# A mixture-of-experts kernel on Trainium2: first expert's index ahead of its low halves, second weights held back, rows of 4160 bytes, six slots transposed by TensorE

## The chip, the cores and the metric

The kernel runs on one core of one Trainium2 chip. The metric is the device time of one execution in microseconds (us). Five engines work side by side, each in the order of its own queue: PE (TensorE, matrix products; PEld is its loading of weights), DVE (VectorE), ACT (ScalarE), POOL (GpSimd, here the issuer of indirect DMAs) and SP (SyncE, the issuer of all other DMAs). An instruction that has to wait stops everything behind it on its engine.

## The reference

Block-local attention (4 batches, 8 heads, 768 positions, 64 channels) gives `x`, 3072 rows of 512. A first expert layer follows: each row goes to one of 8 experts, each takes 384 rows, by a greedy walk over all logits (`flat`, 3072 x 8) in falling order; w1 is 512 x 1024 and w2 1024 x 512 per expert. A second expert layer with a skip gate and a residual ends it.

```python
order = np.argsort(-flat)
for idx in order:
    tok, e = (int(idx) // E, int(idx) % E)
    if assigned[tok] >= 0 or counts[e] >= cap:
        continue
    ...
h = np.maximum(x[mask] @ w1[e], 0.0)
out[mask] = h @ w2[e]
```

## The kernel before, in words

**Precision.** Products are in half precision with a high and a low half: `w1h`, `w1l` are the halves of w1, `hh`, `hl` those of the hidden rows. A product needs three passes: high x high, low x high, high x low. ACT makes the high halves of the weights (L672), DVE the low halves (L675).

**The greedy walk** (`Route.phase`). The experts are closed one after the other. For each, a search of six levels finds the threshold: DVE compares all rows with a level's thresholds (`cmp`, L465), PE counts (L489, L499, L503), DVE takes the next digit (`dg`, `df`, `thr`). At its end `s` (L529) names the expert that closes. From it come `ei` (L547, which lets SP load that expert's weights), masks `bo` (L600), 24 small products on PE (L603), a copy (L606) and an addition (L607) that gives `idx`, the expert's 384 row numbers.

**One expert of the first layer** (`Moe1`). `weights` (L654) loads w1 and w2 in eight pieces of 512 KB into the buffers `wst`, w1 first. `gather` (L678) fetches the rows by three indirect DMAs on POOL (L684, 128 rows each, into `xg`) and transposes them: by DMA (L685), but for expert 0 by PE (L689), with half of each block copied by ACT (L691) and half by DVE (L692). `ffn` (L695) makes eight blocks: `ph` (L708, 3 x 4 products, in two PSUM buffers in turn), `hh` by ACT (L711), `hl` by DVE (L712); then the products `py` (L722) with w2, copied to `yt` (L726). A row of `yt` is 512 values in halves, 512 values and two numbers: 1026 floats, 4104 bytes. It is written to `ysc` in DRAM (L771), and the rows go to `out` by a scatter (L645).

**The second layer** (`Moe2`). List A has six slots of 128 rows, which can start before the last two experts are done, list B the rest. `slot` (L932) gathers rows of `ysc` into `xg` (L934), transposes them by DMA on SP (L940), makes `ph` (L951), `hh`, `hl` (L955), `py` (L962), adds the residual into `xg` (L966) and scatters to `out`. `xg` has four buffers, so a slot's gather waits for the scatter of the slot four before it.

**What sets the order.** All of this is recorded as operations and put in order by a list scheduler (`Sched`): each has an estimated duration, a priority and a correction from a table (`BIAS2` for the expert part) by engine, stage and name. The resulting order of each engine is what runs. Semaphores are set by what an operation reads and writes, not by the table. The key `after` in `weights` is such an estimate only: w2 loads of expert 0 wait for nothing on the chip but their buffers.

Of the kernel before, what the change touches and what calls it, by code (L numbers as in the profile page):

```python
# [427 lines left out]
class Route:  # L428
# [220 lines left out]
class Moe1(Ops):  # L649
# [27 lines left out]

    def gather(self, k, idx, P):  # L678
# [3 lines left out]
        for i in range(3):  # L682
            xg=t([128,1026],F32,"xg",bufs=4); xb=xg.bitcast(F16)[:,:1024]
            self.s.op('POOL',1.1,[idx.name]+[('xscr',c) for c in range(24)],[xg.name],lambda xb=xb,i=i: nc.gpsimd.indirect_dma_start(out=xb,out_offset=None,in_=self.xscr,in_offset=bass.IndirectOffsetOnAxis(ap=idx[:,i:i+1],axis=0)),P-1,dma=.73)  # L684
            if k: self.s.op('SP',.65,[xg.name],[(x.name,i)],lambda xb=xb,i=i: nc.sync.dma_start(x[:,:,128*i:128*i+128],xb,transpose=True),P,dma=1.3)  # L685
            else:
# [338 lines left out]
def build(ctx, tc, i, out, stop=None):  # L1025
# [61 lines left out]
```

## Time and profile before

| | us |
|---|---|
| three runs | 809.8, 813.09 (median), 820.53 |
| profiled execution, own time | 810.57 |
| its span in the profile | 808.7 |
| mean granted PE clock | 0.932 of full speed |

All times of the profile count from the start of the span. A row of a timeline gives the start, the duration, engine, line, operation, what is written and read, and how many instructions it joins; in brackets the idle time of the engine ahead of it and what ended that. The attention ends at about 220 us, the expert part takes the rest.

### The profile page before, as it was taken

How to read it: one execution, taken by the hardware profiler on the slowest of the kernel's cores; microseconds unless marked ns; L12 is line 12 of the kernel's file. 1: busy time of each engine (PE TensorE's matmuls, PEld its weight loads, DVE VectorE, ACT ScalarE, POOL GpSimd, SP SyncE). 2: the span in 40 equal slices, each digit the busy share in tenths (PEclk: the TensorE clock that was granted, in tenths of full speed). 3: DMA queues.
4: the chain of work that ended last, by engine and by line, in shares of the span. 5: the costliest groups of instructions: out<-in, count | busy, mean ns of one | idle time of the engine just before them, and what ended most of it. 6: DMA issues, size and time to landing. Idle time of an engine off the chain costs nothing. (4 is left out here: it accounts for less than half of the span.)

```text
span 808.7 us, 21735 instructions
## 1 busy us (share of the span) xinstructions
PE 698.8 (86%) x8411; PEld 476.8 (59%) x8411; DVE 620.3 (77%) x1875; ACT 402.6 (50%) x777; POOL 229.7 (28%) x233
## 2 busy tenths in 40 slices
PE   3899998978636979998999889799899989999792
PEld 2688877866534545554546454445576657776671
DVE  7888988897685888998999889666569576855740
ACT  3889997864412351525252526452533445646320
POOL 2775866631302011111111113202021132222210
PEclk9999999998755988999999999899999999999997
DMA  8767779691424094868696869999995898898910
GB/s 234 195 162 232 209 215 262 127 175 38 119 90 158 14 300 109 275 169 271 156 266 188 258 183 315 248 298 327 261 220 113 332 344 220 270 324 273 289 31 6
DMA packets 172672, 167.36 MB, mean 207 GB/s; under 512 B 85237, under 2 KB 133365, under 8 KB 172560
## 3 DMA queue, kind: packets, MB, share of 16 engines
q1 hardware_dynamic: 164688, 143.83, 64.6%
q0 software_dynamic: 7872, 22.05, 8.2%
q8 instruction: 68, 1.11, 0.6%
q14 instruction: 44, 0.36, 0.1%
HBM read 114.35 MB, written 29.91 MB: 178 GB/s over the span
## 5 line engine op out<-in xcount | busy, mean ns | idle before, releaser
L708 PE MATMUL ph<-xT,w1h 128*128 128x384 f16 x512 | 102.2, 339 | 7.5 <-DMA xT<-xg 5.1
L951 PE MATMUL ph<-xT,w1h 128*128 128x128 f16 x1152 | 90.1, 222 | 11.6 <-DVE hl L955 7.7
L951 PEld LDWEIGHTS <-w1h 128*128 128x128 f16 x1152 | 73.4, 100 | 16.4 <-issue 12.8
L684 POOL DMA_INDIRECT xg<-xscr,idx x24 | 33.3, 1386 | 164.8 <-DVE idx L607 62.4
L722 PE MATMUL py<-w2h,hh 128*128 128x512 f16 x192 | 74.2, 387 | 4.4 <-ACT yt L726 4.4
L722 PE MATMUL py<-w2l,hh 128*128 128x512 f16 x192 | 74.4, 388 | 0.0
L711 ACT ACTIVATE hh<-ph 128x384 f16<-128x384 f32 x64 | 31.3, 489 | 86.3 <-PE ph L708 76.3
L722 PE MATMUL py<-w2h,hl 128*128 128x512 f16 x192 | 73.9, 385 | 0.0
L708 PEld LDWEIGHTS <-w1h 128*128 128x128 f16 x512 | 48.0, 101 | 41.3 <-issue 15.3
L645 POOL DMA_INDIRECT out<-xg,oid x18 | 29.4, 1636 | 127.4 <-DVE xg L966 69.0
L925 DVE SCALAR_TENSOR_TENSOR w1l<-wst,w1h 128x1024 f16<-128x1024 f32 x44 | 52.0, 1220 | 10.6 <-ACT w1h L924 9.6
L308 ACT ACTIVATE a<-sc,nb 128x120 f32<-128x120 f32 x192 | 53.9, 383 | 12.1 <-DVE nb L306 8.2
L954 ACT ACTIVATE hh<-ph 128x512 f16<-128x512 f32 x36 | 21.3, 593 | 74.6 <-PE ph L951 70.4
L672 ACT ACTIVATE w1h<-wst 128x1024 f16<-128x1024 f32 x32 | 33.5, 1053 | 47.8 <-DMA wst<-moe_w 47.6
L951 PE MATMUL ph<-xT,w1l 128*128 128x128 f16 x576 | 56.9, 222 | 0.0
L645 POOL DMA_INDIRECT out<-yt,dni x24 | 28.0, 1167 | 101.4 <-DVE dw L757 62.2
L925 DVE SCALAR_TENSOR_TENSOR w2l<-wst,w2h 128x1024 f16<-128x1024 f32 x44 | 52.8, 1221 | 4.7 <-ACT w2h L924 2.8
L722 PEld LDWEIGHTS <-hh 128*128 128x128 f16 x384 | 34.0, 101 | 37.2 <-issue 8.1
L962 PE MATMUL py<-w2h,hl 128*128 128x512 f16 x144 | 54.6, 379 | 1.2 <-DVE hl L955 1.0
L708 PE MATMUL ph<-xT,w1l 128*128 128x384 f16 x256 | 54.6, 338 | 0.0
L962 PE MATMUL py<-w2l,hh 128*128 128x512 f16 x144 | 54.6, 379 | 0.0
L962 PE MATMUL py<-w2h,hh 128*128 128x512 f16 x144 | 54.6, 379 | 0.0
(346 smaller groups left out, 1811.0 us busy)
## 6 DMA issues: line engine op xcount, KB each, us to landing
wst<-moe_w SPq DMA_DIRECT2D x152, 512.0 KB
ysc<-yt SPq DMA_DIRECT2D x8, 1539.0 KB
kn<-k SPq DMA_DIRECT2D x24, 256.0 KB
vn<-v SPq DMA_DIRECT2D x24, 256.0 KB
qn<-q SPq DMA_DIRECT2D x24, 256.0 KB
xscr<-xs SPq DMA_DIRECT2D x24, 256.0 KB
W<-vs SPq DMA_DIRECT2D x32, 145.1 KB
W<-vs SPq DMA_DIRECT2D x32, 120.9 KB
```

The lines of the kernel that those rows point to most:

```text
L308: for h in range(4): nc.scalar.activation(a[:,h],sc[:,h],AF.Exp,bias=nb[:,h:h+1],scale=0.125)
L645: s=self.nc.gpsimd.indirect_dma_start(out=self.out,out_offset=bass.IndirectOffsetOnAxis(ap=idx,axis=0),in_=x,in_offset=None,bounds_check=3 ...
L672: self.act(1080,[st.name],[hk],lambda st=st,h=h: nc.scalar.activation(h,st,AF.Copy,scale=32.),P)
L684: self.s.op('POOL',1.1,[idx.name]+[('xscr',c) for c in range(24)],[xg.name],lambda xb=xb,i=i: nc.gpsimd.indirect_dma_start(out=xb,out_offs ...
L708: nc.tensor.matmul(ph[:,:384],a[:,kc,fs],b[:,kc],start=(n==0),stop=(n==11))
L711: self.act(384,[ph.name],[(hh.name,fb)],lambda ph=ph,fb=fb: nc.scalar.activation(hh[:,fb],ph[:,:384],AF.Relu),P+.1)
L722: nc.tensor.matmul(py,a[:,fb,sl],b[:,fb],start=(n==0),stop=(n==23))
L925: self.dve(1024,[st.name,hk],[lk,(lk,0),(lk,1)],lambda st=st,h=h,l=l: V.scalar_tensor_tensor(l,st,16.,h,op0=ALU.mult,op1=ALU.subtract),P-.2)
L951: nc.tensor.matmul(ph[:,128*fi:128*fi+128],w[:,kc,fs],x[:,kc],start=(n==0),stop=(n==11)); n+=1
L954: self.act(512,[ph.name],[(hk,q)]+before(H,q),lambda p4=p4,o=o: nc.scalar.activation(o,p4,AF.Relu),P)
L962: nc.tensor.matmul(py,x[:,fb],w[:,fb],start=(n==0),stop=(n==23))
```

## The change

1. For expert 0 the 24 products of L603 are recorded in two parts (18 and 6). For all experts one reduction (L608 of the new text) replaces copy and addition. All `w1l` of expert 0 read the index, so they come after it.
2. In front of expert 0's w2 loads DVE copies one element of the third gather's buffer into `wst` (L665 new). The load writes the same buffer and so waits for it.
3. Rows of `xg`, `yt`, `ysc` get 1040 floats (4160 bytes). POOL clears the 14 added columns of `yt` (L718 new), and the write of `ysc` waits for that.
4. Expert 0's transposed rows are copied from PSUM by ACT alone.
5. Six slots (list A) are transposed by PE, half of each copied by ACT and half by DVE.
6. Estimates of the scheduler and the whole table `BIAS2` have new numbers, so the order changes on every engine of the expert part.

```diff
-        pe(1.1,[(bo.name,a) for a in range(4)]+[va.name+'a',va.name+'b'],[pI.name],f,P)
-        i6=t([128,6],F32,"i6"); idx=t([128,3],I32,"idx",bufs=3)
-        dve(6,[pI.name],[i6.name],lambda: V.tensor_copy(i6,pI[:,:6]),P)
-        dve(3,[i6.name],[idx.name],lambda: V.tensor_add(idx,i6[:,:3],i6[:,3:]),P)
+        for c0,c1 in ((0,18),(18,24)) if k==0 else ((0,24),):
+            def f(c0=c0,c1=c1):
+                for c in range(c0,c1): nc.tensor.matmul(pI[:,:6],bo[:,c//6,:,c%6],va[:,c],start=(c==0),stop=(c==23))
+            pe((c1-c0)*.046,[(bo.name,a) for a in range(c0//6,c1//6)]+[va.name+'a',va.name+'b']+([pI.name+'p'] if c0 else []),[pI.name if c1==24 else pI.name+'p']+([] if c0 else [pI.name]),f,P)
+        idx=t([128,3],I32,"idx",bufs=3)
+            with nc.allow_low_precision("row numbers"): V.reduce_sum(idx,pI[:,:6].rearrange("p (b a) -> p a b",b=2),axis=AX.X)
+        dve(6,[pI.name],[idx.name],f,P)
...
+            if after and j==4:
+                self.dve(1,[after.name],[st.name,('after',k)],lambda st=st: nc.vector.tensor_copy(st[:1,:1],after[:1,:1]),P)
-            self.s.op('SP',.65,[ei.name]+(list(after) if j>3 else []),[st.name],f,P,dma=1.46)
+            self.s.op('SP',.65,[ei.name]+([('after',k)] if after and j>3 else []),[st.name],f,P,dma=1.46)
-                self.dve(512,[st.name,hk],[(lk,q)],lambda st=st,h=h,l=l,sl=sl: nc.vector.scalar_tensor_tensor(l[:,sl],st[:,sl],32.,h[:,sl],op0=ALU.mult,op1=ALU.subtract),P)
+                self.dve(600,[st.name,hk]+list(idx),[(lk,q)],lambda st=st,h=h,l=l,sl=sl: nc.vector.scalar_tensor_tensor(l[:,sl],st[:,sl],32.,h[:,sl],op0=ALU.mult,op1=ALU.subtract),P)
...
-            xg=t([128,1026],F32,"xg",bufs=4); xb=xg.bitcast(F16)[:,:1024]
+            xg=self.last=t([128,1040],F32,"xg",bufs=4); xb=xg.bitcast(F16)[:,:1024]
-                self.act(512,[px.name],[(x.name,i,'h')],lambda p8=p8,i=i: nc.scalar.activation(x[:,:4,128*i:128*i+128],p8[:,:4],AF.Copy),P)
-                self.dve(512,[px.name],[(x.name,i)],lambda p8=p8,i=i: nc.vector.tensor_copy(x[:,4:,128*i:128*i+128],p8[:,4:]),P,.52)
+                self.act(1080,[px.name],[(x.name,i)],lambda p8=p8,i=i: nc.scalar.activation(x[:,:,128*i:128*i+128],p8,AF.Copy),P)
...
+        yt=t([128,3,1040],F32,"yt",bufs=1)
+        self.pool(42,[],[(yt.name,'z')],lambda: nc.gpsimd.memset(yt[:,:,1026:],0.),P)
...
+        yb=yg.bitcast(F16)[:,:1024]; yks=[yk]
+        if first:
+            yks=[yk,yk+('h',)]; px=ps.tile([128,4,128],F32,"px"); p8=px.bitcast(F16).rearrange("p a (b c) -> p (a b) c",b=2)
+            def f():
+                for c in range(8): nc.tensor.transpose(p8[:,c],yb[:,128*c:128*c+128],C['idh'])
+            self.pe(.45,[yg.name],[px.name],f,P-1.1)
+            self.act(512,[px.name],[yk+('h',)],lambda: nc.scalar.activation(yT[:,:4],p8[:,:4],AF.Copy),P-1.1)
+            self.dve(512,[px.name],[yk],lambda: V.tensor_copy(yT[:,4:],p8[:,4:]),P-1.1,.64)
+        else: self.s.op('SP',.65,[yg.name],[yk],lambda: nc.sync.dma_start(yT,yb,transpose=True),P-1.1,dma=1.85)
...
-    'DVE hl': 234.47, 'DVE i': -6.05, 'DVE idx': -73.76, 'DVE m': -87.83, 'DVE mm': -44.86, 'DVE mq': -67.28, 'DVE need': -60.38, 
+    'DVE g': 70.26, 'DVE ga': -5.11, 'DVE gh': -10.58, 'DVE gm': -14.55, 'DVE gp': 84.61, 'DVE gq': -4.55, 'DVE gw': -0.22, 'DVE hl': 475.4, 
```

DVE from expert 0's masks `bo` on, first before and then now (`i` and `idx` are the copy and the index, `w1l` low halves of w1):

```order
L600 TENSOR_TENSOR bo_5399<-i_141,bb_5395 128x768 x4
L675 SCALAR_TENSOR_TENSOR w1l_5415<-wst_5421,w1h_5413 128x512 x2
L675 SCALAR_TENSOR_TENSOR w1l_5415<-wst_5422,w1h_5413 128x512
L606 COPY i_5400<-cnt_5341 128x6
L675 SCALAR_TENSOR_TENSOR w1l_5415<-wst_5422,w1h_5413 128x512
L607 TENSOR_TENSOR idx_5402<-i_5400 128x3
```

Now:

```order
L600 TENSOR_TENSOR bo_5399<-i_141,bb_5395 128x768 x4
L578 SCALAR_TENSOR_TENSOR mm_5377<-mq_5375,m_5373 128x24
L580 SCALAR_TENSOR_TENSOR ea<-mq_5375,s_5339,ea 128x24
L456 TENSOR_REDUCE wm_243<-w_241 128x24
L583 TENSOR_TENSOR need<-need,cnt_5342 128x8
L457 TENSOR_TENSOR oh_245<-w_241,wm_243 128x192
L608 TENSOR_REDUCE idx_5400<-cnt_5341 128x3
L465 TENSOR_TENSOR cmp_246<-mm_5377,g_133 128x756 x2
```

The four `w1l` ahead of the index are behind it now, and five short operations have come in between.

DVE in expert 0's blocks, at the first low half `hl` of its hidden rows, before (L712) and then now (L716); `w2l` are low halves of w2, `cmp` a level of expert 1's search:

```order
L465 TENSOR_TENSOR cmp_246<-mm_5377,thr_5352 128x372 x2
L518 SCALAR_TENSOR_TENSOR pb_5350<-dg_5346,pb_5349 128x1
L712 SCALAR_TENSOR_TENSOR hl_5432<-ph_5433,hh_5431 128x384
L525 TENSOR_TENSOR gp_5356<-g_136,pb_5350 128x31
L497 CAST cc_5429<-cnt_5342 124x32
L675 SCALAR_TENSOR_TENSOR w2l_5419<-wst_5425,w2h_5417 128x512
```

Now (six of the eight `w2l` and two levels stand further up):

```order
L680 SCALAR_TENSOR_TENSOR w2l_5417<-wst_5426,w2h_5415 128x512
L505 TENSOR_REDUCE dg_5346<-cnt_5341 128x1
L519 TENSOR_REDUCE df_5348<-cnt_5341 128x1
L680 SCALAR_TENSOR_TENSOR w2l_5417<-wst_5426,w2h_5415 128x512
L514 SCALAR_TENSOR_TENSOR thr_5352<-dg_5346,gp_5355 128x31
L521 SCALAR_TENSOR_TENSOR sl_5358<-cnt_5341,df_5348,sl_5357 128x8
L465 TENSOR_TENSOR cmp_246<-mm_5377,thr_5352 128x372 x2
L518 SCALAR_TENSOR_TENSOR pb_5350<-dg_5346,pb_5349 128x1
L716 SCALAR_TENSOR_TENSOR hl_5430<-ph_5431,hh_5429 128x384
```

The first `hl` was ahead of all `w2l` of expert 0 and is now behind the last of them.

DVE at expert 1's index, before and then now:

```order
L600 TENSOR_TENSOR bo_5399<-i_141,bb_5396 128x768 x4
L465 TENSOR_TENSOR cmp_246<-mm_5378,g_133 128x756
L712 SCALAR_TENSOR_TENSOR hl_5432<-ph_5434,hh_5431 128x384
L675 SCALAR_TENSOR_TENSOR w1l_5416<-wst_5421,w1h_5414 128x512
L606 COPY i_5401<-cnt_5342 128x6
L497 CAST cc_5429<-cnt_5341 126x16
L675 SCALAR_TENSOR_TENSOR w1l_5416<-wst_5421,w1h_5414 128x512
L607 TENSOR_TENSOR idx_5403<-i_5401 128x3
```

Now:

```order
L680 SCALAR_TENSOR_TENSOR w1l_5414<-wst_5420,w1h_5412 128x512
L502 TENSOR_TENSOR sat_5343<-cnt_5341,need 128x8
L680 SCALAR_TENSOR_TENSOR w1l_5414<-wst_5420,w1h_5412 128x512
L680 SCALAR_TENSOR_TENSOR w1l_5414<-wst_5421,w1h_5412 128x512 x2
L680 SCALAR_TENSOR_TENSOR w1l_5414<-wst_5422,w1h_5412 128x512 x2
L505 TENSOR_REDUCE dg_5345<-cnt_5341 128x1
L519 TENSOR_REDUCE df_5347<-cnt_5341 128x1
L608 TENSOR_REDUCE idx_5401<-cnt_5342 128x3
```

Between `bo` and the index of expert 1 stood two `w1l`; now it is all eight, one of them ahead of `bo`.

## Rows read from the trace of the kernel before

**Rows 1.** The page: busy time, share of the span, instructions of each engine

```profile
PE 698.8 (86%) x8411; PEld 476.8 (59%) x8411; DVE 620.3 (77%) x1875; ACT 402.6 (50%) x777; POOL 229.7 (28%) x233
```

**Rows 2.** Windows: stretch, length, busy PE, PEld, DVE, ACT, POOL; PE clock, DMA, GB/s

```profile
240.00:260.00 20.00, 10.69 (x83) 8.05 (x83) 12.67 (x40) 5.65 (x7) 4.23 (x3) 0.50 0.54 200
```

**Rows 3.** Timeline of DVE at the start of expert 0

```profile
238.97 1.95 DVE L600 TENSOR_TENSOR bo<-i,bb 128x768 f16<-128x768 f16 x4
...
243.32 0.14 DVE L607 TENSOR_TENSOR idx<-i 128x3 int32<-128x3 f32 x1
...
252.67 0.42 DVE L692 COPY xT<-px 128x512 f16<-128x512 f16 x1 [3.31 <-ACT xT L691]
...
254.34 1.79 DVE L465 TENSOR_TENSOR cmp<-mm,thr 128x756 f16<-128x756 f32 x2
```

**Rows 4.** Timeline of PE at the start of expert 0

```profile
239.56 1.85 PE L603 MATMUL cnt<-va,bo 128*128 128x6 f16 x24 [2.88 <-DVE bo L600]
...
250.97 1.03 PE L689 MATMUL px<-idh,xg 128*128 128x128 f16 x8 [2.77 <-DMA xg<-xscr,idx]
...
256.85 1.44 PE L708 MATMUL ph<-xT,w1h 128*128 128x384 f16 x4
```

**Rows 5.** Timeline of POOL: first and third gather of expert 0

```profile
244.53 1.67 POOL L684 DMA_INDIRECT xg<-xscr,idx  x1 [30.17 <-ACT w1h L672]
...
248.01 1.36 POOL L684 DMA_INDIRECT xg<-xscr,idx  x1 [0.30 <-issue]
```

**Rows 6.** The gathers of line 684, from issue to landing

```profile
DMA to landing us min/median/max: 4.1/5.3/6.5
```

**Rows 7.** Timeline of SP: expert 0's w2 loads

```profile
238.15 2.33 SPq L667 DMA_DIRECT2D wst<-moe_w  x4
```

**Rows 8.** Timeline of DVE in expert 0's blocks, up to expert 1's index

```profile
260.14 0.99 DVE L465 TENSOR_TENSOR cmp<-mm,thr 128x372 f16<-128x372 f32 x2
...
261.49 0.56 DVE L712 SCALAR_TENSOR_TENSOR hl<-ph,hh 128x384 f16<-128x384 f32 x1 [0.29 <-ACT hh L711]
...
263.04 0.68 DVE L675 SCALAR_TENSOR_TENSOR w2l<-wst,w2h 128x512 f16<-128x512 f32 x1
...
279.09 0.15 DVE L529 TENSOR_REDUCE s<-sl 128x1 f32<-128x8 f32 x1
...
289.44 0.14 DVE L607 TENSOR_TENSOR idx<-i 128x3 int32<-128x3 f32 x1
```

**Rows 9.** Timeline of PE from expert 0's last products to expert 1's first

```profile
292.25 0.54 PE L722 MATMUL py<-w2h,hh 128*128 128x512 f16 x1 [2.33 <-ACT yt L726]
...
302.60 0.95 PE L489 MATMUL cnt<-oh,cmp 128*124 128x32 f16 x6 [1.41 <-DVE cmp L465]
...
304.67 2.72 PE L708 MATMUL ph<-xT,w1h 128*128 128x384 f16 x8
```

**Rows 10.** Timeline of POOL: gathers and scatters of list A's slots

```profile
555.73 0.99 POOL L934 DMA_INDIRECT xg<-ysc,rowsA  x1 [28.03 <-DVE rowsA L880]
...
613.87 0.99 POOL L645 DMA_INDIRECT out<-xg,oid  x1 [6.96 <-DVE dd L847]
618.09 1.14 POOL L934 DMA_INDIRECT xg<-ysc,rowsA  x1 [3.23 <-DMA out<-xg,oid]
```

**Rows 11.** Timeline of SP: transposes of list A, write of the seventh expert

```profile
561.48 5.11 SPq L940 DMA_TRANSPOSE xT<-xg  x2
566.68 0.63 SPq L771 DMA_DIRECT2D ysc<-yt  x1
```

**Rows 12.** Timeline of ACT: the last expert's first copy to `yt`

```profile
578.36 0.60 ACT L726 ACTIVATE yt<-py 128x512 f32<-128x512 f32 x1 [4.22 <-DMA ysc<-yt]
```

**Rows 13.** Timeline of PE at the same place

```profile
579.01 0.58 PE L722 MATMUL py<-w2h,hh 128*128 128x512 f16 x1 [2.10 <-ACT yt L726]
```

**Rows 14.** The page's groups: busy, mean ns of one, idle before and what ended it

```profile
L722 PE MATMUL py<-w2h,hh 128*128 128x512 f16 x192 | 74.2, 387 | 4.4 <-ACT yt L726 4.4
```

**Rows 15.** Timeline of PE: the longest wait for a transposed block

```profile
508.95 2.72 PE L708 MATMUL ph<-xT,w1h 128*128 128x384 f16 x8 [4.39 <-DMA xT<-xg]
```

More of the change, by code (lines that the diff above doesn't have):

```diff
@@ L652, in __init__, with weights @@
         self.__dict__.update(d)
-    def weights(self, k, ei, P, after=()):
+    def weights(self, k, ei, P, after=None, idx=()):
         nc=self.nc; t=self.wk.tile
@@ L697, in ffn @@
         xh,xl=x[:,:4],x[:,4:]; w1h,w1l,w2h,w2l=w
-        xk=[(x.name,i) for i in range(3)]+([(x.name,i,'h') for i in range(3)] if k==0 else [])
+        xk=[(x.name,i) for i in range(3)]
         hh=t([128,8,384],F16,"hh",bufs=1); hl=t([128,8,384],F16,"hl",bufs=1)
@@ L735, in score @@
             self.dve(512,[(yt.name,i),(yt.name,'h',i)],[(yt.name,'l',i)],lambda y=y,b=b: nc.vector.scalar_tensor_tensor(b[:,512:],y,1024.,b[:,:512],op0=ALU.mult,op1=ALU.subtract),P+.15)
[L736 removed]
+            self.s.op('SP',.65,[(yt.name,'h',i),(yt.name,'l',i)],[yT.name],lambda b=b,yT=yT: nc.sync.dma_start(yT,b,transpose=True),P+.15,dma=1.85)
             pc=ps.tile([128,512],F32,"cnt") if k==7 else ps.tile([128,4,128],F32,"px").rearrange("p a b -> p (a b)")
@@ L769, in decide @@
         dve(3,[cm.name,(yt.name,'t')],[ni.name],lambda: V.scalar_tensor_tensor(ni,cm,65536.,yt[:,:,1025],op0=ALU.mult,op1=ALU.add),P)
-        yk=[(yt.name,x) for x in (0,1,2,'g','t')]+[(yt.name,x,i) for x in 'hl' for i in range(3)]
+        yk=[(yt.name,x) for x in (0,1,2,'g','t','z')]+[(yt.name,x,i) for x in 'hl' for i in range(3)]
         self.s.op('SP',.65,yk,[('ysc',k)],lambda: nc.sync.dma_start(self.ysc[384*k:384*k+384].rearrange("(i p) d -> p i d",p=128),yt),P,dma=4.38)
@@ L951, in f @@
                             nc.tensor.matmul(ph[:,128*fi:128*fi+128],w[:,kc,fs],x[:,kc],start=(n==0),stop=(n==11)); n+=1
-                self.pe(.68,[yk]+[(w.name,j) for w in (w1h,w1l) for j in range(4)]+([] if fi==0 else [ph.name+str(fi-1)]),[ph.name+str(fi) if fi<3 else ph.name]+([ph.name] if fi==0 else []),f,P)
+                self.pe(.68,yks+[(w.name,j) for w in (w1h,w1l) for j in range(4)]+([] if fi==0 else [ph.name+str(fi-1)]),[ph.name+str(fi) if fi<3 else ph.name]+([ph.name] if fi==0 else []),f,P)
             o=hh[:,4*q:4*q+4]; ol=hl[:,4*q:4*q+4]; p4=ph.rearrange("p (f d) -> p f d",f=4)
@@ L1030, in build @@
     dp=ctx.enter_context(tc.tile_pool(name="dp",bufs=1,space=bass.MemoryType.DRAM))
-    xscr=dp.tile([3072,1024],F16,name="xscr"); ysc=dp.tile([3072,1026],F32,name="ysc")
+    xscr=dp.tile([3072,1024],F16,name="xscr"); ysc=dp.tile([3072,1040],F32,name="ysc")
     wb=Rot(ctx,tc,"wb",2)
@@ L1045, in route, with weights @@
         def route(k): R[k]=r.phase(k,2.0*k,last=(k==7))
-        def weights(k,after=()): W[k]=m.weights(k,R[k][1],2.0*k+5,after)
+        def weights(k,after=None,idx=()): W[k]=m.weights(k,R[k][1],2.0*k+5,after,idx)
         def fetch(k): G[k]=m.gather(k,R[k][0],2.0*k+3.15)
-        S.stage='a'; route(0); fetch(0); weights(0,[(G[0].name,2)])
+        S.stage='a'; route(0); fetch(0); weights(0,m.last,[R[0][0].name])
         S.stage='b'; route(1); weights(1); fetch(1)
```

86 lines of the change are left out of this document (42 added, 44 removed).

## The prediction

> **What bounds the kernel now.** I read the page's busy times first [rows 1]: TensorE (PE) works 86% of the span, VectorE (DVE) 77%. PE's own work is a floor that the change does not lower, so only PE's idle places and its slow places can give anything. The second view is the timeline of the engines where the expert part starts, since expert 0 is the one place where nothing older is left for PE. The window there [rows 2] shows PE busy 10.69 of 20 us at a granted clock of 0.50, the lower level of 1.2 GHz. The third view, PE's own waits further on, shows gaps of one to four us and no single long one.
>
> At the start the reader is to see a chain. DVE ends the four `bo` at 238.97 + 1.95 = 240.92. PE's 24 products end at 241.41 [rows 4]. The index is ready only at 243.46 [rows 3], because low halves (`w1l`) lie in between. The first gather does not start then either, but at 244.53, because GpSimd (POOL) waited for ACT's `w1h` [rows 5]. Its rows are on PE at 250.97, 6.4 us later, and expert 0's first product `ph` runs at 256.85 [rows 4].
>
> **The index and the gathers.** In the new order the reduction of L608 follows `bo` after five short operations, and no `w1l` is ahead of it. Those five stood ahead of `bo` before. The index cannot be much earlier than PE's products: 241.4 + 0.15 if `bo` does not move, and up to 0.9 earlier if `bo` moves up by all that the five took. I take 241.1, a gain of 2.4 (1.9 to 2.8). The nine waits that the first gather had are now on the memset of L718 ahead of it, so I let the gather start 0.3 behind the index, at 241.4: 3.1 earlier. If the memset still waits for a high half, up to 1.1 of that is lost. The third gather started 3.48 after the first [rows 5]; it is issued at 244.9. A gather lands after 4.1 to 6.5, median 5.3 [rows 6]; the one that can be read here took 6.4, with the w2 loads issued at 238.15 beside it [rows 7]. Without them I take 4.9: landing at 249.8 (249.0 to 251.4). Eight transposes at this clock take 1.03 [rows 4]. ACT's whole copy I put at 1.0, an estimate from DVE's half copy of 0.42 [rows 3] with a bound of 0.8 to 1.2. First `ph`: about 252 (250.9 to 253.6), against 256.85. Expert 0 starts 4.8 earlier.
>
> **What is late next.** The same reordering moves other things. First, the 1x1 copy that holds back the w2 loads stands in DVE's queue between two `w1l`, with the second level of the search behind it. Between index and copy DVE has one `cmp` pair (1.7 from its start to the next row, [rows 3]), five `w1l` of 0.6 and some 1.6 of short operations, so it is there at about 247.5 and stands until 249.8. The second level's `cmp`, at 254.34 before [rows 3], comes at about 250.5: still 3.5 earlier. Second, and this I hold for the larger cost: the first `hl` of expert 0 stood ahead of `w2l` (261.49 and 263.04, [rows 8]). Now it stands behind all eight `w2l` and three search levels. PE has two `ph` buffers, so the third block of expert 0 cannot start before that `hl`. The first two blocks are six groups of four products at about 1.25 each, 1.44 with the last one's end [rows 4], with 1.5 of search products between: PE is through at about 261. On DVE, the third level's `cmp` was at 260.14 [rows 8]; its counts now wait for the same two blocks on PE, so I put it at 259. From there to `hl` it is three `cmp` pairs of 0.92, eight `w2l` of 0.6 (each 0.6 to 0.68, [rows 8]) and some 1.5 of short operations: 2.8 + 4.8 + 1.5 = 9.1, so 268. PE stands from 261 to 268, less about 2.5 of search products in it: 4.5 lost, nearly all of the 4.8 gained.
>
> Third, expert 1. Its search should end earlier, since its counts no longer queue behind `ph` on PE in levels three to five: `s` at about 276 against 279.09 [rows 8]. But before, two `w1l` stood between `s` and the index, 10.35 us; now it is eight, 6 x 0.6 = 3.6 more, one more `hl` (0.5) and about 0.9 of other work: 15.3. The index comes at about 291.4 against 289.44. Expert 1's first `ph` was at 304.67, behind waits of 2.33 and 1.41 [rows 9] that can absorb this. From PE's side it could come 2 to 3 earlier, from the index's side 1 to 2 later. For the whole start I take -0.5. Bounds: -4.8 (all is kept) and +4 (the idle 4.5 at `hl` stays and the lower clock goes on behind it).
>
> **Six slots by TensorE.** Added on PE: 6 x 8 transposes. At the granted clock of 0.50 eight took 1.03; at full clock half of it, 0.5: +3.0 (up to 6). ACT and DVE have room for six copies each. The last of them, slot 5, waits for a gather that waits for slot 1's scatter. Before, that gather started 4.2 after the scatter was issued [rows 10], and a gather of `ysc` follows; PE has some 11 of other products in between. Chain: 0.8 + 0.3 + 4.2 + 0.3 + 5.8 to 8.1 = 11.4 to 13.7, so 0.4 to 2.7 of standing; I take 0.5, its lower end, since the first of these gathers took under 6 to the transposes behind it (555.7 to 561.5, [rows 10, 11]). Removed: six DMA transposes from SP's queue. There two issues held SP 5.11 from 561.48, and behind them the write of `ysc` came only at 566.68 [rows 11]. ACT waited 4.22 for it, [rows 12], and PE 2.10 at 579.01 [rows 13]; that product took 0.58 where its group's mean is 0.387 [rows 14]; some seven like it follow, and I put 1.5 on them. I take the whole of these 3.6 as saved: 3.0 + 0.5 - 3.6 = -0.1. Bounds: -2 (PE places the transposes in gaps) and +6 (nothing saved, lower clock behind the standing).
>
> The Trainium skill speaks against this edit: its page "Advanced Engine Details and Errata", section "X-Bar Transpose (TRN2)", says that transpose DMAs are as fast as regular ones on this chip. By that rule taking them off SP frees next to nothing, and the sum of this part would be +3.5. The trace does not agree where it counts: two transposes of 256 KB held SP 5.11 us, while four loads of 512 KB took 2.33 [rows 7, 11].
>
> **Rows of 4160 bytes, memsets.** Bytes rise by 1.4%. Each memset stands ahead of the next gathers on POOL and waits until the last expert's `yt` is written out and transposed; POOL works 28% of the span [rows 1], and the gathers that follow wait for an index of their own. I take 0; bounds -2 (row starts that suit the memory better) and +1 (a memset that stands). All numbers of the order being new, the rest of the expert part is shuffled; gaps like the 4.39 at 508.95 [rows 15] may go or come. Value 0, bounds +-5.
>
> **Sum.** 810.57 (span 808.7 and 1.9 around it) - 0.5 - 0.1 = 810.0. The median of the three runs is 813.09, inside their scatter (809.8 to 820.53); I forecast from the profiled execution's own time.
>
> **Rivals.** (a) The gain is kept. If `hl` is reached before PE has ended two blocks, or search levels shrink enough, expert 1 starts 4.8 earlier; and with SP relieved the wait for a transposed `xT` at 508.95 (4.39) goes too: 810.6 - 4.8 - 0.6 - 4.4 = 800.8. For it: both waits are real PE idle time. Against it: the order of DVE, in which nothing shortens the way to `hl`. (b) Slower: `hl` behind the `w2l`. The w2 loads start only at 250; if their high halves come late, each `w2l` stands too, `hl` comes at 271 or later, and PE goes on at the lower clock: a group of four `ph` at 1.25 instead of about 0.65 for some ten groups is 6 more. 810.0 + 6.5 = 816.5. It decides from the point where `hl` comes later than about 268. Against it: the loads have no neighbours then. (c) The change does not do what it says: the first gather still waits for a high half and its rows still take 6.4, so the copy stands until 252 and the search gains nothing: 812.5.
>
> **How the numbers follow.** My forecast (806 to 814): 0.5. Rival (a): 0.22; (b): 0.2; (c): 0.08. The range takes in (a), (b) and most of the shuffle: 798 to 820. About 2%, or 16 us, is what a measurement of this kernel can tell from no change: below 794 only (a) with a lucky shuffle, 0.1; above 827 (b) with an unlucky one, 0.05; within, 0.85.
>
> **What would show it.** In the profile after: the first gather at 241 to 242, the first `ph` at 251 to 254; an idle stretch of PE of 3 to 7 before expert 0's third block, ended by DVE `hl`; expert 1's index 14 to 16 behind its `s`; no wait of ACT `yt` for `ysc` at the seventh expert. I am wrong if expert 0's blocks run through without that stretch, or if expert 1's first `ph` comes before 301 or after 309.

## The result, and the profile after

| | before | changed |
|---|---|---|
| median, us (six runs each) | 812.94 | 792.53 |
| lowest to highest | 809.61 to 820.53 | 788.92 to 795.4 |
| profiled execution, own time | 810.57 | 788.92 |
| its span | 808.7 | 787.0 |
| mean granted PE clock | 0.932 | 0.940 |

Some executions of a kernel take over 1.5% longer than its quickest; the ratios leave those out. The ratio is 0.9743 with a 95% interval of [0.9693, 0.9793]: 2.6% faster. The forecast was no change, 810.0 us, with a range of 798 to 820; the time lies below it.

The page of the changed kernel, busy times and (its group line) the products `py`, the answers to [rows 1] and [rows 14]:

```profile
PE 693.7 (88%) x8459; PEld 481.0 (61%) x8459; DVE 618.1 (79%) x1871; ACT 406.7 (52%) x783; POOL 233.1 (30%) x241
...
L727 PE MATMUL py<-w2h,hh 128*128 128x512 f16 x192 | 72.6, 378 | 0.0
```

PE is busy 5.1 us less though it has 48 transposes more (8459 matmuls against 8411): a product `py` took 378 ns on average instead of 387, at a granted clock of 0.940 instead of 0.932. Its idle time fell from 109.9 (808.7 - 698.8) to 93.3 (787.0 - 693.7), and that is most of the 21.7 us.

The start, the answers to [rows 2] to [rows 5] and [rows 8]. First the window, then POOL, PE and DVE:

```profile
240.00:260.00 20.00, 13.70 (x110) 9.58 (x108) 15.19 (x53) 10.82 (x12) 4.11 (x3) 0.62 0.69 236
```

```profile
242.31 1.59 POOL L689 DMA_INDIRECT xg<-xscr,idx  x1 [24.23 <-DVE idx L608]
...
245.59 1.43 POOL L689 DMA_INDIRECT xg<-xscr,idx  x1 [0.30 <-issue]
```

```profile
251.76 1.75 PE L712 MATMUL ph<-xT,w1h 128*128 128x384 f16 x5 [1.11 <-ACT xT L696]
...
261.97 0.95 PE L489 MATMUL cnt<-oh,cmp 128*124 128x32 f16 x6 [1.87 <-DVE cmp L465]
...
266.01 0.95 PE L489 MATMUL cnt<-oh,cmp 128*124 128x32 f16 x6 [1.87 <-DVE cmp L465]
...
267.01 1.44 PE L712 MATMUL ph<-xT,w1h 128*128 128x384 f16 x4
...
304.27 1.46 PE L712 MATMUL ph<-xT,w1h 128*128 128x384 f16 x8 [2.02 <-DMA xT<-xg]
```

```profile
241.85 0.16 DVE L608 TENSOR_REDUCE idx<-cnt 128x3 int32<-128x6 f32 x1
...
249.59 0.14 DVE L665 COPY wst<-xg 1x1 f32<-1x1 f32 x1 [1.27 <-DMA xg<-xscr,idx]
...
266.40 0.55 DVE L716 SCALAR_TENSOR_TENSOR hl<-ph,hh 128x384 f16<-128x384 f32 x1
...
275.52 0.16 DVE L529 TENSOR_REDUCE s<-sl 128x1 f32<-128x8 f32 x1
...
291.21 0.15 DVE L608 TENSOR_REDUCE idx<-cnt 128x3 int32<-128x6 f32 x1
```

This stretch went nearly as forecast: the first `ph` is 5.1 us earlier than in [rows 4]. PE is through with two blocks at about 258, then does nothing but search products until `hl` comes at 266.40, and starts the third block at 267.01; it is idle for 5.65 us of that stretch. Expert 1's first `ph` is at 304.27, where it was at 304.67 in [rows 9]. So the gain is not made here. Each of the eight experts has 168 products `ph` and `py`. When PE has ended the 336th, 672nd, 1008th and 1344th of them, the changed kernel is 3.4, 6.0, 12.0 and 17.4 us ahead of the kernel before; with the products of the slots counted too it is 20 to 22 us ahead at about 600 us. The gain is made a little at a time, in experts 1 to 6 for the most part, where the forecast had seen nothing.

What differs there is the write of `ysc`. Expert 2's, on the kernel before, SP and then ACT and DVE (the idle time of the last two rows is the wait for the weights and for the write):

```profile
394.04 0.39 SPq L771 DMA_DIRECT2D ysc<-yt  x1
400.13 1.94 SPq L664 DMA_DIRECT2D wst<-moe_w  x4
```

```profile
403.93 1.06 ACT L672 ACTIVATE w1h<-wst 128x1024 f16<-128x1024 f32 x1 [1.25 <-DMA wst<-moe_w]
```

```profile
402.90 0.17 DVE L768 CAST yt<-dtb 128x3 f32<-128x3 int32 x1 [0.47 <-DMA ysc<-yt]
```

The write lands at 402.9, 8.9 us after its issue, and DVE, which wants to put a number into `yt`, stands for it. The same in the changed kernel, where POOL's clearing of the new columns is the first to need `yt`:

```profile
389.76 0.39 SPq L776 DMA_DIRECT2D ysc<-yt  x1
395.05 1.94 SPq L669 DMA_DIRECT2D wst<-moe_w  x4
```

```profile
398.76 1.06 ACT L677 ACTIVATE w1h<-wst 128x1024 f16<-128x1024 f32 x1 [3.23 <-DMA wst<-moe_w]
```

```profile
395.48 0.13 POOL L718 MEMSET yt<- 128x42 f32 x1 [2.38 <-issue]
```

```profile
397.50 0.16 DVE L773 CAST yt<-dtb 128x3 f32<-128x3 int32 x1
```

Here `yt` is free within 5.7 us, and DVE does not wait. Over the seven experts that follow a write the clearing starts 5.6 to 6.7 us after the issue of the write; in the kernel before, DVE's cast started 8.7 to 11.6 after it where it had to wait. The weights' load is issued 5.3 us behind the write instead of 6.1, and ACT's first high half starts 3.7 us behind the load, as before (3.8). Of the waits of [rows 12] and [rows 13] for the seventh expert's write ACT's is 1.45 us and PE's is gone. The wait of [rows 15], on PE, has shrunk too. ACT for the write, then PE:

```profile
560.35 0.60 ACT L731 ACTIVATE yt<-py 128x512 f32<-128x512 f32 x1 [1.45 <-DMA ysc<-yt]
```

```profile
495.42 1.46 PE L712 MATMUL ph<-xT,w1h 128*128 128x384 f16 x8 [2.81 <-DMA xT<-xg]
```

### The profile page after: what moved, and what is told of

Same layout as the page of the kernel before. It is cut to its first block, busy times and chain, and to the rows that moved or that the text cites. A ratio compares the mean times of both kernels' runs of the same rounds, so it can differ in the third digit from the quotient of the medians.

```text
span 787.0 us, 21844 instructions
## 1 busy us (share of the span) xinstructions
PE 693.7 (88%) x8459; PEld 481.0 (61%) x8459; DVE 618.1 (79%) x1871; ACT 406.7 (52%) x783; POOL 233.1 (30%) x241
## 5 line engine op out<-in xcount | busy, mean ns | idle before, releaser
L712 PE MATMUL ph<-xT,w1h 128*128 128x384 f16 x512 | 100.1, 332 | 6.8 <-DMA xT<-xg 5.4
L689 POOL DMA_INDIRECT xg<-xscr,idx x24 | 38.9, 1619 | 125.6 <-DVE x L510 44.6
L727 PE MATMUL py<-w2l,hh 128*128 128x512 f16 x192 | 72.7, 378 | 0.0
L727 PE MATMUL py<-w2h,hh 128*128 128x512 f16 x192 | 72.6, 378 | 0.0
L712 PEld LDWEIGHTS <-w1h 128*128 128x128 f16 x512 | 46.6, 100 | 36.5 <-issue 7.2
L647 POOL DMA_INDIRECT out<-xg,oid x18 | 25.1, 1395 | 117.9 <-DVE xg L979 82.9
L647 POOL DMA_INDIRECT out<-yt,dni x24 | 26.0, 1082 | 110.8 <-DVE dsm L765 34.1
L677 ACT ACTIVATE w1h<-wst 128x1024 f16<-128x1024 f32 x32 | 33.5, 1053 | 44.5 <-DMA wst<-moe_w 44.2
L929 ACT ACTIVATE w1h<-wst 128x1024 f16<-128x1024 f32 x44 | 44.4, 1050 | 22.2 <-DMA wst<-moe_w 19.7
L929 ACT ACTIVATE w2h<-wst 128x1024 f16<-128x1024 f32 x44 | 45.9, 1053 | 18.3 <-PE py L975 11.6
L975 PE MATMUL py<-w2l,hh 128*128 128x512 f16 x144 | 54.6, 379 | 0.0
L975 PE MATMUL py<-w2h,hh 128*128 128x512 f16 x144 | 54.6, 379 | 0.0
```

The source lines that it names most:

```text
L647: s=self.nc.gpsimd.indirect_dma_start(out=self.out,out_offset=bass.IndirectOffsetOnAxis(ap=idx,axis=0),in_=x,in_offset=None,bounds_check=3 ...
L677: self.act(1080,[st.name],[hk],lambda st=st,h=h: nc.scalar.activation(h,st,AF.Copy,scale=32.),P)
L712: nc.tensor.matmul(ph[:,:384],a[:,kc,fs],b[:,kc],start=(n==0),stop=(n==11))
L727: nc.tensor.matmul(py,a[:,fb,sl],b[:,fb],start=(n==0),stop=(n==23))
L929: self.act(1080,[st.name],[hk],lambda st=st,h=h: nc.scalar.activation(h,st,AF.Copy,scale=16.),P-.2)
L975: nc.tensor.matmul(py,x[:,fb],w[:,fb],start=(n==0),stop=(n==23))
```

## The experiments

"The changed kernel with ..." keeps its order on every engine, unless said otherwise. Each run's ratio is against the kernel before, run on the same chip beside it. Compare times within one trace, from one event to another: the expert part itself starts at different times, with the first gather at 238.5 to 242.6 us in the traces of the changed order.

### What each part is worth

**The order, with edits 2, 3 and 5 undone.** Rows of 4104 bytes, no clearing, w2 not held back, six slots transposed by DMA, issued by SP at the place of TensorE's transposes. Edits 1 and 4 stay in.

```diff
-            xg=self.last=t([128,1040],F32,"xg",bufs=4)
+            xg=self.last=t([128,1026],F32,"xg",bufs=4)
...
-                self.dve(1,[after.name],[st.name,('after',k)],lambda st=st: nc.vector.tensor_copy(st[:1,:1],after[:1,:1]),P)
+                self.dve(1,[after.name],[st.name,('after',k)],lambda: None,P)
...
+                if dma: nc.sync.dma_start(yT,yb,transpose=True)
```

> The changed kernel with its order of instructions kept on every engine, but three of its parts undone: rows of 4104 bytes again and no memset, the w2 loads of expert 0 not held back, the six slots transposed by DMA (issued by SP where TensorE's transposes stood). Theory A (the new order made the gain; my step 'the rest is shuffled, value 0' failed): ratio to the kernel before 0.975 to 0.985, 793 to 801 us. Theory B (the parts made it, above all SP and the DMAs relieved of six transposes and the aligned rows): 0.99 to 1.005, 805 to 817 us, and PE's waits for xT come back. Mixed: between.

Measured: 846.84 us, ratio 1.0462 [1.0367, 1.0557]. Both theories missed: the new order without those three edits is much slower than the kernel before.

**Slots by DMA**, all else as changed (the last line of the diff above).

> The changed kernel in its own order, only the six slots transposed by DMA again (SP issues them where TensorE's transposes stood). Theory A: within 3 us of the changed kernel (790 to 796), the standing of TensorE for slot 4's transposed block (2.4 us) goes or becomes a wait for the DMA. Theory B: 4 to 10 us slower (797 to 803), with ysc written late again and ACT's copy to yt waiting for it.

Measured: 803.3 and 808.25 us; two more executions took 816.62 and 816.86, which makes the median 812.43. Up to about 580 us this kernel is as far as the changed one; then PE stands 7.25 and 13.39 us for two transposed slots:

```profile
590.01 1.01 PE L966 MATMUL ph<-xT,w1h 128*128 128x128 f16 x8 [7.25 <-DMA xT<-xg]
...
630.42 1.01 PE L966 MATMUL ph<-xT,w1h 128*128 128x128 f16 x8 [13.39 <-DMA xT<-xg]
```

By the two shorter times the edit is worth about 13 us in this order (11 to 16), more than theory B had. That is not its worth in the order of before, where SP issued the transposes at other places; that was not tried. At the seventh expert ACT stood for the write again, as theory B had it, though the rows have 4160 bytes:

```profile
561.88 1.09 ACT L731 ACTIVATE yt<-py 128x512 f32<-128x512 f32 x2 [5.34 <-DMA ysc<-yt]
```

**Rows of 4104 bytes**, all else as changed (the first two lines of the diff above, the same for `yt` and `ysc`; no clearing).

> The changed kernel in its own order, only the rows at 4104 bytes again, without the memset. My prediction: 0 (790 to 795 us, ratio 0.971 to 0.978). Rival: aligned rows make the gathers and writes of ysc faster, then 3 to 8 us slower (796 to 801) and longer waits behind gathers of ysc in lists A and B.

Measured: 813.82 us (ten runs), ratio 1.0005 [0.9958, 1.0053]. The whole gain is gone with the 56 bytes, far more than the rival had put. Expert 2's write on SP, the weights behind it on ACT, DVE's cast:

```profile
392.33 0.39 SPq L776 DMA_DIRECT2D ysc<-yt  x1
397.63 1.95 SPq L669 DMA_DIRECT2D wst<-moe_w  x4
```

```profile
403.22 1.06 ACT L677 ACTIVATE w1h<-wst 128x1024 f16<-128x1024 f32 x1 [5.12 <-DMA wst<-moe_w]
```

```profile
402.43 0.17 DVE L773 CAST yt<-dtb 128x3 f32<-128x3 int32 x1 [2.27 <-DMA ysc<-yt]
```

The write lands after 10.1 us, and the view of who waited for it has `DVE yt L773: 23.7, 7`: 23.7 us of standing in seven experts, against 2.7 in one. At the seventh expert ACT stands longer than before the change, although PE transposes the slots:

```profile
583.62 0.60 ACT L731 ACTIVATE yt<-py 128x512 f32<-128x512 f32 x1 [6.12 <-DMA ysc<-yt]
```

**w2 of expert 0 not held back** (the second piece of the first diff).

> The changed kernel in its own order, only the w2 loads of expert 0 issued at once behind the w1 loads. Theory of the prediction: gathers take up to 6.4 us to land, so expert 0's first product comes 1 to 2 us later, but DVE no longer stands for the third gather; end 0 to 1 us later, since expert 1 starts by its own index. Rival (holding back costs, DVE stands 1.3 us): 1 to 2 us faster.

Measured: 797.89 us, ratio 0.983 [0.9748, 0.9912]. The hold does what it was put in for: here the first gather's rows were on PE 7.26 us after the gather started, and the first `ph` came after 12.04; in the changed kernel it was 4.75 and 9.45. At expert 1's first `ph` nothing of it is left (304.12 against 304.27, with a first gather 2.2 us earlier). The difference to the changed kernel in the end appears only at about 500 us, and the hold does not explain it. The intervals overlap. It stays open whether the edit is worth anything in the end.

**Before's order with rows of 4160 bytes**, the new columns cleared by DVE behind its cast.

```diff
-        yt=t([128,3,1026],F32,"yt",bufs=1)
+        yt=t([128,3,1040],F32,"yt",bufs=1)
...
-lambda: V.tensor_copy(yt[:,:,1025],tb),P)
+lambda: (V.tensor_copy(yt[:,:,1025],tb),V.memset(yt[:,:,1026:],0.)),P)
```

> The kernel before in its own order, only its rows at 4160 bytes (DVE clears the 14 added columns right behind its copy into yt, 8 small operations more). Theory C (the row pitch itself: the write of ysc lands in about 6 us instead of 9 to 12, so DVE's copy into yt, which waits for it, no longer stands in front of the search and of hl): writes land in 5.5 to 7 us, ratio 0.98 to 0.99, 796 to 805 us. Rival (the pitch helps only in the new order, or only since a memset on POOL takes the wait): 0.995 to 1.005.

Measured: 802.63 us, ratio 0.9892 [0.984, 0.9944]. The width alone gives 1.1% in the order of before; DVE's cast waits 0.2 us in one expert.

### Which property of the rows

**Cleared by DVE, not by POOL**, all else as changed.

```diff
-lambda: nc.gpsimd.memset(yt[:,:,1026:],0.),P)
+lambda: None,P)
...
-lambda: V.tensor_copy(yt[:,:,1025],tb),P)
+lambda: (V.tensor_copy(yt[:,:,1025],tb),V.memset(yt[:,:,1026:],0.)),P)
```

> The changed kernel in its own order, the added columns cleared by DVE behind its copy into yt instead of by POOL ahead of the gathers, so that the wait for the write of ysc is DVE's again. Theory C: DVE waits under 1 us per expert since the write has landed by then; 790 to 796 us. Rival (what helped is that POOL waits in DVE's place): DVE waits 2 to 4 us per expert, 800 to 812 us.

Measured: 791.77 us, ratio 0.9776 [0.9731, 0.9822]. The clearing on POOL neither costs nor gains.

**Rows of 4128 and of 4352 bytes** (in the second 1088 floats for 1040, at the same four places).

```diff
-ysc=dp.tile([3072,1040],F32,name="ysc")
+ysc=dp.tile([3072,1032],F32,name="ysc")
```

> The changed kernel with rows of 1032 floats, 4128 bytes: a multiple of 32, not of 64. If a row start on 64 bytes is what counts: writes of ysc land in 9 to 11 us, 805 to 815 us. If 32 will do: 5.5 to 6.7 us and 790 to 796.

> The changed kernel with rows of 1088 floats, 4352 bytes: a multiple of 256. If only starts on 256 bytes avoid an extra transaction, writes land faster than with 4160 (under 5.4 us) and the time falls 2 to 5 us more. If 64 is enough: 5.5 to 7 us as now, 790 to 797 us.

Measured, one run each: 790.63 and 792.85 us. The clearing starts 5.6 to 6.6 and 5.9 to 7.1 us after the issue. 4128 and 4160 are multiples of 32 bytes, 4352 of 256, 4104 of neither.

**Rows of 4160 bytes in SBUF, 4104 in DRAM.**

```diff
-ysc=dp.tile([3072,1040],F32,name="ysc")
+ysc=dp.tile([3072,1026],F32,name="ysc")
...
-p=128),yt),P,dma=4.38)
+p=128),yt[:,:,:1026]),P,dma=4.38)
```

The slots' gathers read 1026 columns too (a line that is not shown above).

> The changed kernel with rows of 4160 bytes in SBUF (yt and xg) but of 4104 bytes in DRAM (ysc); the added columns are cleared and not written. Theory A, the pitch of the rows in DRAM is what makes the write slow: it lands 8.7 to 12 us after its issue, and the time is that of rows of 4104 bytes, 808 to 818 us. Theory B, the pitch in SBUF is: it lands after 5.5 to 6.7, 789 to 795 us.

Measured: 811.06 us (ten runs), ratio 0.9967 [0.9932, 1.0002]; expert 2's write lands 9.8 us after its issue. So what counts lies on the DRAM side. There the pitch (the distance from one row's start to the next) and the length of each row that is written were always the same number; a run with rows 4160 bytes apart of which 4104 are written would tell the two apart, and there is none.

### How a slow write costs time

**4104 bytes, cast off DVE.** DVE casts into a small buffer; POOL copies it into `yt` just ahead of the write.

```diff
-lambda: V.tensor_copy(yt[:,:,1025],tb),P)
+lambda: V.tensor_copy(tf,tb),P)
...
-lambda: nc.sync.dma_start(self.ysc
+lambda: (nc.gpsimd.tensor_copy(yt[:,:,1025],tf),nc.sync.dma_start(self.ysc
```

> The changed kernel with rows of 4104 bytes again and no clearing of columns (as in rows_4104, 813.8 us), but DVE no longer writes into yt early: its cast (L773) goes into a small buffer of its own, and POOL copies it into yt just ahead of the write of ysc. Theory A, the slow write of ysc costs time because DVE's early cast stands until the write has landed (23.7 us of standing in 7 experts in rows_4104) and everything behind it on DVE with it: most of the loss goes though the write itself stays at 9 to 12 us, 796 to 802 us. Theory B, it costs time through the transfers themselves (gathers, transposes and weights beside a slower write, ACT's copies into yt): 809 to 815 us.

Measured: 826.81 us, ratio 1.0136 [1.0057, 1.0215], slower still: theory A's forecast fell. DVE stands no more, but POOL's copy makes the write later, and the loads follow it by only 3.3 to 4.5 us instead of 5.2 to 5.9. Now ACT stands for them. ACT's groups between 305 and 500 us, here and then in the changed kernel (17 and 24 high halves fall into the window; the last column is the idle time):

```profile
L677 ACT ACTIVATE w1h<-wst 128x1024 f16<-128x1024 f32 x17 | 17.9, 1054 | 37.8 <-DMA wst<-moe_w 37.8
```

```profile
L677 ACT ACTIVATE w1h<-wst 128x1024 f16<-128x1024 f32 x24 | 25.1, 1052 | 17.1 <-DMA wst<-moe_w 16.8 <-issue 0.3
```

That gave the second theory: the write fills the DMA queues, and what is issued behind it pays.

**4160 bytes, cast off DVE** (the same edit, clearing kept).

> The changed kernel (rows of 4160 bytes, POOL's clearing kept) with the same move of the cast: DVE writes it into a buffer of its own, POOL copies it into yt ahead of the write of ysc. Theory A, the quick write leaves nothing to wait for on DVE: only the one stand of 2.7 us goes, 788 to 793 us, the same as the changed kernel. Theory B, DVE's cast still costs in ways the idle column does not show: under 786 us.

Measured: 790.93 us, ratio 0.9717 [0.9651, 0.9783]. With the quick write the same edit, with the same short distance of 3.2 to 4.4 us, costs nothing.

**The write behind the loads.** Cast off DVE; SP issues the write behind the next weights' four w1 loads, first with 4104, then with 4160 bytes, then (4160) behind all eight loads. POOL's copy into `yt` moves behind the scatters with it.

```diff
+        self.s.behind.update({len(self.s.ops):self.s.wl[k+2,3]} if k<6 else {})
...
+        t[i]=max([t[i]]+[t[j] for j in x[2]]+([t[S.behind[i]]+.001] if i in S.behind else []))
```

> As rows_4104_cast_off_dve (826.8 us), but SP issues the write of ysc behind the four w1 loads of the next expert's weights, not 3.3 to 4.5 us ahead of them. Theory A, the slow write costs time because the weights that are issued behind it land only when it is through (there 7.3 to 9.7 us from the loads' issue to ACT's first w1h, 3.5 to 5.2 in the changed kernel): the first w1h comes 3.5 to 4.5 us after the issue again, and the time falls below 812 us, to 798 to 812. Theory B, the weights are late whatever stands ahead of them, or the write's own end is what counts (the next yt, the gathers): 820 us or more.

> As cast_off_dve (rows of 4160 bytes, 790.9 us), with the write of ysc behind the next expert's four w1 loads. Theory A, with the quick write there is little left to win: first w1h 3.5 to 4 us after its load's issue instead of 3.5 to 5.2, 786 to 791 us. Theory B, the later write holds yt longer and the gathers with it: over 793 us.

> As cast_off_dve (rows of 4160 bytes, 790.9 us), with the write of ysc behind all eight loads of the next expert's weights. Theory A: w1 and w2 land as early as they can, 784 to 791 us. Theory B: the write ends some 11 us later, POOL's clearing waits for it and stands ahead of the next gathers: 795 us or more.

Measured: 852.8 us, ratio 1.0552 [1.0451, 1.0652]; 816.32, 1.0044 [0.9999, 1.0088]; 829.38, 1.0216 [1.0157, 1.0275]. The first `w1h` came 3.6 to 4.4 us after its load again, as theory A had it; the times it forecast were all far off. With 4104 bytes the w2 loads are now the ones behind the write. SP, ACT, DVE and PE in that kernel:

```profile
319.04 1.96 SPq L669 DMA_DIRECT2D wst<-moe_w  x4
321.12 0.56 SPq L776 DMA_DIRECT2D ysc<-yt  x1
321.88 4.83 SPq L672 DMA_DIRECT2D wst<-moe_w  x4
```

```profile
339.18 1.06 ACT L677 ACTIVATE w2h<-wst 128x1024 f16<-128x1024 f32 x1 [9.56 <-DMA wst<-moe_w]
...
342.61 0.61 ACT L739 ACTIVATE yt<-yt 128x512 f16<-128x512 f32 x1
```

```profile
343.25 0.69 DVE L740 SCALAR_TENSOR_TENSOR yt<-yt 128x512 f16<-128x512 f32 x1 [10.88 <-ACT yt L739]
```

```profile
344.68 0.20 PE L499 MATMUL cnt<-cc,sel 126*128 126x8 f16 x2 [10.71 <-DVE cc L497]
```

The first w2 half came 17.3 us after its load was issued. ACT stood for it, the copy of `yt` (L739) stood behind it on ACT, DVE behind that copy (10.88 us), PE behind DVE. With all eight loads ahead the weights are in time, and whoever needs `yt` pays: the view of who waited for the write has `POOL yt L718: 87.0, 5` and `ACT yt L731: 46.5, 7`. With 4160 bytes something else comes in. POOL's clearing waits for the write, and the next expert's gathers stand behind the clearing, here with the write behind w1:

```profile
335.30 0.14 POOL L718 MEMSET yt<- 128x42 f32 x1 [15.64 <-DMA ysc<-yt]
336.06 1.02 POOL L689 DMA_INDIRECT xg<-xscr,idx  x1 [0.62 <-issue]
```

So none of the places tried was free. For the two kernels with 4160 bytes that may lie in the clearing's place ahead of the gathers; no run moved the write with the clearing elsewhere.

**Written twice.** Rows of 4160 bytes, each `yt` written a second time to rows that nobody reads.

```diff
-lambda: nc.sync.dma_start(self.ysc[384*k:384*k+384]
+lambda: [nc.sync.dma_start(z[384*k:384*k+384]
...
+ for z in (self.ysc,self.ysd)]
```

> The changed kernel (rows of 4160 bytes) with each expert's yt written to DRAM twice, the second time to rows of 4160 bytes that nobody reads. Theory A, what a slow write costs is its length in the DMA queues, paid by whatever is issued behind it (the next weights) and by whoever needs yt next: the two writes land 10 to 12 us after the issue, as one write with rows of 4104 bytes does, ACT's first w1h comes 6 us or more after its load's issue, and the time is 808 to 825 us. Theory B, the row starts themselves matter (for the gathers that read them, or in the memory): two quick writes cost little, under 800 us.

Measured: 828.79 us, ratio 1.0068 [1.0035, 1.0101] (the kernel before took 823.55 beside it, so the ratio is what counts). Theory A holds: without any change of the rows the long write alone gives the gain back, and more. Expert 2's second write lands 10.2 us after its issue; DVE stands 35.7 us for the second writes and POOL 60.0, in seven experts each.

One table for the eleven kernels that bear on this, from the SP and ACT timelines of the first five writes of each; the fourth column is the time from the first write to the fifth, divided by four:

| kernel | first load behind the write | first `w1h` behind its load, mean | write to write | ratio |
|---|---|---|---|---|
| before | 6.1 to 8.0 | 4.77 | 39.88 | 1 |
| before, 4160 bytes | 6.1 to 8.0 | 3.79 | 39.19 | 0.9892 |
| changed | 5.2 to 6.0 | 4.14 | 37.78 | 0.9743 |
| changed, 4104 bytes | 5.2 to 5.9 | 6.69 | 39.87 | 1.0005 |
| changed, 4104 in DRAM alone | 5.3 to 6.0 | 6.17 | 39.62 | 0.9967 |
| 4160, cast off DVE | 3.2 to 4.4 | 5.02 | 37.80 | 0.9717 |
| 4104, cast off DVE | 3.3 to 4.5 | 8.63 | 42.70 | 1.0136 |
| 4160, written twice | 5.2 to 6.1 | 7.81 | 43.21 | 1.0068 |
| 4160, write behind w1 | -2.1 | 3.78 | 42.69 | 1.0044 |
| 4160, write behind all loads | -4.5 to -5.2 | 3.88 | 45.79 | 1.0216 |
| 4104, write behind w1 | -2.1 | 3.81 | 49.65 | 1.0552 |

The changed order puts the next weights closer to the write. With a quick write each expert is 2.1 us shorter than before; with a slow one the weights slip by 2.5 us and the experts are as long as before. In the changed order with 4104 bytes DVE stands and the weights are late at once. The kernel that took away the one made the other worse, so how the loss divides between the two is not shown.

### The forecast stands

**The first `hl` early.** Expert 0's first two `hl` moved up on DVE, as soon as what they read was begun.

```diff
+            (k==0 and fb<2) and self.s.early.add(len(self.s.ops))
...
+        t[i]=d if i in S.early else max(t[i]+S.late.get(i,0.),d)
```

> The changed kernel with the first two low halves hl of expert 0 moved up on DVE, ahead of a level and of the last low half of w2; nothing else moves. Theory A, the stand of PE in expert 0's blocks is swallowed at expert 1's first products, which wait for its index and its transposed rows: the two stands of 1.87 us at 262 and 266 us shrink, expert 1's first ph still comes at 303 to 305 us, time 790 to 795 us. Theory B, the start of expert 0 carries through: expert 1's first ph 2 us or more earlier and 787 to 790 us.

Measured: 792.68 us, ratio 0.974 [0.9673, 0.9807]. Expert 1's first `ph` is at 303.18, after a wait of 2.08 us for its transposed rows; that is 64.62 us behind the first gather, against 61.96 in the changed kernel, so nothing of the early `hl` is left: theory A. PE's stands at the search products stayed at 1.87 each, though; they belong to the search.

**Slot 5 later.** The eight transposes of the sixth slot 6 us later in PE's order.

```diff
+            self.s.late.update({len(self.s.ops):6.} if self.slots==5 else {})
```

> The changed kernel with the eight transposes of list A's sixth slot 6 us later in PE's order, behind 14 groups of other products. Theory A, the stand of 2.44 us at 613 us is a wait for the slot's gather and lost time for PE: it goes, 787 to 791 us. Theory B, the time is made up behind it (an expert's or a slot's other waits come next): same as the changed kernel, 790 to 795 us.

Measured: 791.7 us, ratio 0.9735 [0.9656, 0.9814]. The stand did not go: it was 3.24 us here. It was never a wait for that slot's gather, as ACT in the changed kernel and then PE show:

```profile
611.42 1.06 ACT L929 ACTIVATE w1h<-wst 128x1024 f16<-128x1024 f32 x1 [12.35 <-DMA wst<-moe_w]
612.38 1.07 ACT L951 ACTIVATE xT<-px 128x512 f16<-128x512 f16 x2
```

```profile
613.01 0.61 PE L964 MATMUL ph<-xT,w1h 128*128 128x128 f16 x8 [2.44 <-ACT xT L951]
```

The transposes were done at 610.6; ACT's copies stood in its queue behind a high half that waited for its weights.

**All small steps together**: rows of 4128 bytes, cast off DVE, `hl` early, slot 5 later.

> The changed kernel with the small steps together: rows of 4128 bytes, the cast off DVE, the first two hl of expert 0 early, slot 5's transposes 6 us later. Theory A, each was within its scatter of the changed kernel and they stay so together: 787 to 793 us. Theory B, they add: 782 to 787 us.

Measured: 794.16 us (six runs), ratio 0.9652 [0.9602, 0.9702], beside 823.55 for the kernel before. By its time it is the changed kernel again, by its ratio a little better; the changed kernel did not run beside them, so a gain is not shown.

## Why the prediction was wrong

**Index and gathers: right.** Index 241.85 (241.1 was said), first gather 242.31 (241.4), third 245.59 (244.9), w2 held until 249.59 (249.8), first `ph` 251.76 (252). The start of the expert part lies up to 4 us apart between traces, so part of this closeness is luck. What does not depend on it is the way from the first gather to the first `ph`: 9.45 us, where the forecast had 10.6 and the kernel before 12.32. The kernel without the hold needed 12.04, so that is the hold.

**What is late next: right.** First `hl` 266.40 (268), `s` 275.52 (276), expert 1's index 291.21 (291.4), PE idle for 5.65 us ahead of the third block (4.5), expert 1's first `ph` 304.27, 0.4 earlier than before (0.5 was put). Moving `hl` up changed nothing: expert 1 waits for its own rows. The two signs that were to show the forecast wrong, blocks that run through and a first `ph` of expert 1 outside 301 to 309, did not come; they looked at the start alone, and the gain came behind it.

**Six slots by TensorE: half of the reason.** The transposes cost what was put: sixteen took 1.06 us. The standing was put at 0.5 for a gather; it was 2.44, and it came from ACT's queue. The wait of ACT for `ysc` (4.22), which was counted as saved because SP would be relieved, fell to 1.45. In the changed order that took both edits: it was 6.12 with slots by TensorE and 4104 bytes, and 5.34 with 4160 bytes and slots by DMA. In the order of before the 4160 bytes alone did it (ACT then stood 1.49 us, and for PE). Nor were the 5.11 us that two transposes held SP the rule: of the 18 at L940 half held it 1.35 us or less, the longest 8.11. Counting the edit as -0.1 also missed that the new order leans on it: taking it out of that order costs about 13 us.

**Rows of 4160 bytes: the step that failed.** "I take 0; bounds -2 (row starts that suit the memory better) and +1". The bracket looked at the right place, the rows in DRAM, and its bound was too small by far: 7.9 us in the order of before (802.63 against 810.54), 21 in the new one (813.82 against 792.53). The bound was made without pricing the transfer. The trace of before held the price of the old one: the write landed 8.7 to 11.6 us after its issue where DVE had to wait for it, with the DMA engines full. What 4160 bytes would bring, no row of before could tell; it showed how much time there was to lose. The window from the write to the loads behind it, in the kernel before, in the changed one and with 4104 bytes in the changed order (the last two columns are the DMA share and GB/s):

```profile
394.10:399.50 5.40, 5.40 (x45) 3.33 (x43) 4.31 (x25) 0.98 (x2) 3.38 (x3) 1.00 0.99 233
```

```profile
389.80:395.00 5.20, 5.20 (x44) 3.23 (x42) 4.11 (x24) 0.98 (x2) 2.69 (x3) 1.00 0.80 308
```

```profile
392.40:397.60 5.20, 5.20 (x43) 3.21 (x42) 4.11 (x24) 0.98 (x2) 2.65 (x3) 1.00 1.01 226
```

PE, DVE and ACT do the same in all three; the DMA engines are full at 226 to 233 GB/s with 4104 bytes, and idle a fifth of the time at 308 with 4160.

**The shuffle: wrong in kind.** "Value 0, bounds +-5" took the new order for noise. The parts do not add: the width alone gives 1.1%, all but the width nothing (1.0005), the order without the width, the hold and the transposes costs 4.6%, and all together gain 2.6%. That the order was made with a quick write in mind is my reading; that it needs one is shown by the table.

**The rivals.** (a) named a time of 800.8, but its mechanism, a start that is kept, did not happen; only its wait at 508.95 shrank, from 4.39 to 2.81. (b) and (c) did not happen.

## What to carry to other kernels

Price every transfer whose shape a change touches from its landing time and from the DMA share of that window, not from its bytes: 1.4% more bytes made this write land in about 6 us instead of 9 to 12. Where the new shape has no price yet, try it alone before the whole change is forecast. A long DMA is paid by what is issued behind it and by what waits for its buffer, so a stand removed on one engine, or the DMA put elsewhere, may come back larger elsewhere. Where a list of priorities is refitted together with the edits, forecast the whole, since a part can be worth several times as much in one order as in another (7.9 us and 21 here).

## What the runs showed of the hardware

The shape of the rows in DRAM (their pitch and length, which went together in every run) set the speed of a write of 384 rows of about 4.1 KB. In the changed kernel and its copies with 4128 and 4352 bytes `yt` was free within 5.6 to 7.1 us of the issue; with 4104 bytes it took 8.7 to 12, from an SBUF pitch of 4160 bytes too. 4128 bytes, a multiple of 32 and not of 64, were enough. Neighbours count as well: with 4160 bytes and w2 loads issued 0.6 us behind the write `yt` was free only after 11.0 to 12.6 us, and with 4128 bytes and w1 loads 3.6 us behind it once after 8.4 (the kernel with all small steps). Why the 4104 bytes are slow is not shown by any run. The Trainium skill's "DMA: Bandwidth & Descriptors", section "How a descriptor splits into AXI transactions", has a transaction that reads start at a 256-byte boundary. That is told of reads, and a multiple of 256 bytes brought nothing here: 4352 was no quicker than 4128 and 4160. The Trainium skill's "Collectives: The Full Stack", section "Rules for kernel authors", wants buffers aligned to 32 bytes so that the hardware need not read, modify and write. That is said of collectives; it fits these times, but no run shows that it is the cause.
